# A GeGLU feed-forward kernel: the weights of contraction slice 0 in four transfers, and the opening products in another order

## The chip, the core and the metric

The kernel runs on one core of one Trainium2 chip. A core has TensorE (matrix products, PE in the profile), VectorE (DVE), ScalarE (ACT), GpSimd (POOL) and SyncE (SP), each with its own instruction stream; they meet only at semaphores. Transfers between the chip's memory (HBM) and the core's memory (SBUF) are issued by SP, ACT and POOL and run on 16 DMA engines that all queues share. Matrix products write into PSUM, which has 8 banks. The metric is the device time of one execution in microseconds; less is better.

## The reference

Input `x` is 32 x 32 x 1024, so N = 1024 tokens of D = 1024 values; `w_gate` and `w_up` are 1024 x 3584, `w_down` is 3584 x 1024, all bfloat16.

```python
def reference(x, w_gate, w_up, w_down):
    return (_gelu(x @ w_gate) * (x @ w_up)) @ w_down
```

`_gelu` is the tanh form. The first two products contract over D, the last over F = 3584.

## The kernel before

**Tiling.** D is cut into DK = 8 contraction slices of 128 (the index `dk`; "chunk" in the change's own words), F into 28 blocks of 128 (index `m`). A product instruction takes a 128 x 128 block of weights (loaded into the array by a LDWEIGHTS, PEld in the profile) and streams 128, 256 or 512 tokens of `xT`, the transposed input, through it. A *part* is one block `m` for one range of tokens; its gate product G and its up product U each sum over the 8 slices in PSUM. Parts 0 to 7 are blocks 0 to 7 for tokens 0 to 255, each with one PSUM bank of its own (G in one half, U in the other); parts 8 to 15 are the same blocks and banks for tokens 256 to 511; all parts after that are 512 tokens wide. When a part is summed, ScalarE applies the gelu to G into one of four buffers (line 443), and VectorE multiplies it with U into `hT` (line 483), which frees the bank. After the last part the down product runs (line 421).

**Opening.** The order of TensorE's instructions is a list, `steps`, written out at lines 157 to 184, and each instruction waits just for what it reads. First come ten warm-up products on constants (`WARM`, line 393: six of 512 columns, four of 128), which need no data. Then `turn_xa` (line 345) turns the first 256 tokens (two blocks `b` of 128) for slices 0 to 4: ten 128 x 128 products with an identity matrix (line 351), which go to PSUM in four pieces (`XA_PS`, line 131) and are copied to `xT` by ScalarE (line 436). VectorE turns slices 5 to 7 of the same tokens itself (line 459). Then TensorE runs slice 0 of parts 0 to 7 (line 174: G of parts 0, 1, 2, 6, 3, 7, 4, then U of 0 to 3, G of 5, U of 7, 6, 4, 5), then slices 1 to 5 of all eight parts (`together(range(0, 8), 1, 6)`), then slices 6 and 7 in two halves of four parts, slice 7 part by part so that the parts end one after another.

**Tokens 256 to 511.** Slices 0 to 3 of parts 8 to 11 are first done for tokens 256 to 383 (`XB1`), then for tokens 384 to 511 (`XB2`), because VectorE is still turning these tokens (line 474). VectorE's own order is the string `mix` at line 188: `E3` is the multiply that ends part 3, `A0` to `A3` turn slices 0 to 3 of XB1, `B` those of XB2, `D` slices 4 to 7 of both, `C` tokens 512 to 1023. VectorE, like every engine here, works strictly in that order.

**Loads.** SP issues the first 128 tokens of x, then the weights of blocks 0 to 7 as 16 transfers of 256 KB in the order gate, up for slice 0, gate, up for slice 1 and so on (`load_w0`, line 288; 128 rows of 2 KB each, one semaphore each). ACT issues the other 128 tokens. When the up weights of slice 5 have landed (line 300), SP and ACT issue the rest of x in pieces XB1, XB2 and XC2. All of SP's transfers are served by one queue in their order. The other weight blocks are loaded in groups of four blocks when the x pieces have landed or a buffer is free.

**The extra wait.** `HOLD` (line 132, used at line 379) makes U of part 6 in slice 5 wait for the gate weights of slice 7, two slices before they are read.

Of the kernel before, what the change touches and what calls it, by code (L numbers as in the profile page):

```python
# [5 lines left out]
P = 128  # L6
# [78 lines left out]
def bass_standalone__geglu_ffn__sampling_kernel(  # L85
# [13 lines left out]
    DK = D // P  # L99
# [7 lines left out]
    NBIG = 8  # L107
    GSZ = 4
# [20 lines left out]
    XB1, XB2 = (256, 384), (384, 512)  # L129
    XPIECES = [XB1, XB2, XC2]  # L130
    XA_PS = [(3, 0, 1, 0, 1), (7, 0, 1, 1, 2), (4, 1, 3, 0, 2), (5, 3, 5, 0, 2)]
    HOLD = ((6, "U", 5), ("wg", 7))
    XA_DVE = (5, 8)


# [21 lines left out]
    steps = []  # L157

    def together(ps_, k0, k1, tok=None):
        for dk in range(k0, k1):  # L160
            for key in ("G", "U"):
                for p in ps_:
                    steps.append((p, key, dk, tok))

    def one_by_one(ps_, k0):
        for p in ps_:
            for key in ("G", "U"):
                for dk in range(k0, DK):
                    steps.append((p, key, dk, None))

    for k0, k1 in ((0, 3), (3, XA_DVE[0])):
        for b in range(2):
            steps += [("X", b, dk) for dk in range(k0, k1)]
    for key, ps_ in (("G", (0, 1, 2, 6, 3, 7, 4)), ("U", (0, 1, 2, 3)), ("G", (5,)), ("U", (7, 6, 4, 5))):
        steps += [(p, key, 0, None) for p in ps_]
    together(range(0, 8), 1, 6)
    for half in (range(0, 4), range(4, 8)):
        together(half, 6, 7)
        one_by_one(half, 7)
    together(range(8, 12), 0, 4, XB1)  # L180
    together(range(8, 12), 0, 4, XB2)
    together(range(8, 12), 4, 6)
    one_by_one(range(8, 12), 6)
# [1 line left out]


    dve_order = []
    mix = ("E0 E1 E2 A0 E3 A1 A2 A3 B0 B1 B2 B3 E4 D4 D5 E5 D6 D7 E6 E7 "
           "C0 E8 C1 E9 C2 E10 E11 C3 C4 E12 C5 E13 C6 C7 E14 E15")
    for w in mix.split():  # L190
        if w[0] == "E":
# [14 lines left out]
    def evac_eng_is_act(ji):  # L206
# [9 lines left out]
    C_PE = _Clock("pe")  # L216
    C_ACT = _Clock("act")
    C_DVE = _Clock("dve")
    C_POOL = _Clock("pool")
    Q_XA = [_Clock(f"xa{b}", 16) for b in range(2)]  # L220
    Q_X = {(q, s): _Clock(f"x{i}{s}", 16) for i, q in enumerate(XPIECES) for s in range(2)}
    Q_W0 = {(w, k): _Clock(f"{w}0k{k}", 16) for k in range(DK) for w in ("wg", "wu")}
    Q_WG = [_Clock(f"wg{j}", 16) for j in range(NG)]
    Q_WU = [_Clock(f"wu{j}", 16) for j in range(NG)]
    Q_WD_SP = _Clock("wd_sp", 16)
    Q_WD_POOL = _Clock("wd_pool", 16)
    Q_OUT = _Clock("out", 16)
    all_clocks = [C_PE, C_ACT, C_DVE, C_POOL, *Q_XA, *Q_X.values(), *Q_W0.values(), *Q_WG, *Q_WU,
                  Q_WD_SP, Q_WD_POOL, Q_OUT]

    ctx = _Ctx()

    with ExitStack() as es:
        def sb(name, shape, dtype):
            return es.enter_context(nc.sbuf_tensor(name, shape, dtype))
# [9 lines left out]
        big = {w: sb(w + "big", [P, DK, NBIG * P], BF16) for w in ("wg", "wu")}  # L245
        small = {w: sb(w + "small", [P, DK, GSZ * P], BF16) for w in ("wg", "wu")}
        w_r = {"wg": wg_r, "wu": wu_r}
# [13 lines left out]
        def wbuf(w, buf):  # L261
            if buf == "s":
                return small[w]
            o = 0 if buf == "lo" else GSZ * P
            return big[w][:, :, o:o + GSZ * P]
# [15 lines left out]
        def load_x(ew, eng, q, side):  # L281
            c0, c1 = q[0] // 32, q[1] // 32
            for a in (2 * side, 2 * side + 1):
                v = ew.do(lambda: eng.dma_start(
                    xs[32 * a:32 * (a + 1), c0:c1, :], x_r[a, :, c0:c1, :]), clock=Q_X[(q, side)])
            ctx.set(("x", q, side), v)

        def load_w0(ew, eng, w, k):
            ctx.set((w + "0", k), ew.do(lambda: eng.dma_start(
                big[w][:, k, :], w_r[w][:, k, 0:NBIG * P]), clock=Q_W0[(w, k)]))  # L290

        def early_loads(ew, eng, side):
            ctx.set(("xa", side), ew.do(lambda: eng.dma_start(
                xa[:, side, :], xa_r[:, side, :]), clock=Q_XA[side]))
            yield
            if side == 0:
                for k in range(DK):
                    for w in ("wg", "wu"):
                        load_w0(ew, eng, w, k)
            ew.wait(Q_W0[("wu", 5)], ctx.get(("wu0", 5)))  # L300
            for q in XPIECES:
                load_x(ew, eng, q, side)

# [22 lines left out]
        def prog_sp(eng):  # L326
            sp = _Eng(ctx, eng, None)
            for _ in early_loads(sp, eng, 0):
                pass
            wd_mine = [k for k in range(len(wd_groups)) if k % 2 == 0]  # L330
            for j in range(NG):
                known_chunk = gate_w(sp, j)
                load_w(sp, eng, "wg", j)
                issue_wd(sp, eng, wd_mine, known_chunk, Q_WD_SP)
            issue_wd(sp, eng, wd_mine, FM, Q_WD_SP, force=True)
            ctx.set("wd_sp_total", Q_WD_SP.n)
            last = None
            for ji, (tc, col0, ncols, b) in enumerate(jobs):
                sp.wait(C_ACT if evac_eng_is_act(ji) else C_DVE, ctx.get(("E", ji)))
                last = sp.do(lambda: eng.dma_start(  # L340
                    out_r[:, tc, col0:col0 + ncols],
                    osb[:, tc, col0:col0 + ncols]), clock=Q_OUT)
            sp.wait(Q_OUT, last)
# [14 lines left out]
        def part_step(pe, eng, opened, i, key, dk, tok):  # L358
            m, t0, t1, gs, us = parts[i]
            w, (bank, f0, f1) = ("wg", gs) if key == "G" else ("wu", us)  # L360
            if tok is not None:
                f0, f1 = f0 + tok[0] - t0, f0 + tok[1] - t0
                t0, t1 = tok
            buf, slot, j = slot_of[m]
            if j is None:
                pe.wait(Q_W0[(w, dk)], ctx.get((w + "0", dk)))
            else:
                pe.wait((Q_WG if w == "wg" else Q_WU)[j], ctx.get((w, j)))
            if bank in bank_before[i]:
                pe.wait(C_DVE, ctx.get(("D", bank_before[i][bank])))  # L370
            for jx, (xbank, k0, k1, _b0, _b1) in enumerate(XA_PS):
                if t0 == XA[0] and (xbank == bank or k0 <= dk < k1):
                    pe.wait(C_ACT, ctx.get(("XA", jx)))
            if t0 == XA[0] and dk >= XA_DVE[0]:
                pe.wait(C_DVE, ctx.get("XD"))
            for q in XPIECES:
                if q[0] < t1 and t0 < q[1]:
                    pe.wait(C_DVE, ctx.get(("T", dk, q)))
            if (i, key, dk) == HOLD[0]:
                pe.wait(Q_W0[HOLD[1]], ctx.get((HOLD[1][0] + "0", HOLD[1][1])))  # L380
            first = (i, bank) not in opened
            opened.add((i, bank))
            last = (dk == DK - 1)
            v = pe.do(lambda: eng.matmul(  # L384
                ps[:, bank, f0:f1],
                wbuf(w, buf)[:, dk, slot * P:(slot + 1) * P],
                xT[:, dk, t0:t1],
                start=first, stop=last and (key == "U" or gs[0] != us[0]),
            ), mark=last)
            if last:  # L390
                ctx.set((key, i), v)

        WARM = [512] * 6 + [128] * 4

        def prog_pe(eng):
            pe = _Eng(ctx, eng, C_PE)
            for n in WARM:
                pe.do(lambda: eng.matmul(ps[:, 0, 0:n], ones_w, ones_x[:, 0:n],  # L398
# [3 lines left out]
            for step in steps:  # L402
                if step[0] == "X":
                    turn_xa(pe, eng, *step[1:])
                else:
                    part_step(pe, eng, opened, *step)
# [134 lines left out]
```

## Time and profile before

| what | value |
|---|---|
| median of 3 runs | 299.04 us (298.87 to 299.05) |
| the profiled execution | 299.08 us, of which the profile's span is 297.8 us; 1.28 us lie around it |
| TensorE products | busy 293.9 us, 99% of the span |
| LDWEIGHTS | 148.1 us, 50% (beside the products) |
| VectorE / ScalarE / GpSimd | 64.3 / 42.3 / 7.9 us |
| DMA | 26.43 MB, 89 GB/s over the span |

The profile names a group of instructions by engine, line of the code, and output and inputs. A line with "idle before" in square brackets says how long the engine was idle just ahead and what ended that. Products are pipelined: a product of 256 columns is shown for 0.27 us, but its successor starts 0.109 us later, so it is the starting times that tell the pace.

### The profile page before, as it was taken

The page shows a single profiled execution, that of the slowest core. Times are in us where ns is not written, and L with a number is a line of the kernel's source. Part 1 is how long each engine was busy: PE and PEld are TensorE (multiplying, and loading weights), DVE is VectorE, ACT ScalarE, POOL GpSimd, SP SyncE. Part 2 cuts the span into 40 slices and gives each one's busy share as a digit, 9 for nine tenths or more (in the row PEclk, how much of TensorE's full clock was granted, in tenths as well). Part 3 has the DMA queues.
Part 4 walks back from the last instruction along what each step waited for, and adds up shares of the span by engine and source line. Part 5 has one row for each costly group of instructions (what it writes and reads, how often), then busy time and mean ns, then how long its engine had stood idle before and what let it go on. Part 6 is the DMA issues. An engine that isn't in the chain of part 4 may idle for free.

```text
span 297.8 us, 3492 instructions
## 1 busy us (share of the span) xinstructions
PE 293.9 (99%) x1528; PEld 148.1 (50%) x1552; DVE 64.3 (22%) x108; ACT 42.3 (14%) x79; POOL 7.9 (3%) x14
## 2 busy tenths in 40 slices
PE   8999999999999999999999999999999999999997
PEld 5899644444444444444444444444444444444445
DVE  4669721111122111122111112110000000000000
ACT  4032211121111121111112111110000000000000
POOL 1001001020000002001000000000000000000000
PEclk9999999999999999999999999999999999999999
DMA  7997104856009301942003000000000100010001
GB/s 248 392 207 233 52 2 139 284 199 227 0 0 298 127 0 34 371 161 110 33 0 141 0 2 0 0 0 20 18 18 20 35 18 18 20 35 18 18 20 35
DMA packets 17806, 26.43 MB, mean 89 GB/s; under 512 B 1152, under 2 KB 11392, under 8 KB 17792
## 3 DMA queue, kind: packets, MB, share of 16 engines
q1 hardware_dynamic: 13840, 16.78, 17.0%
q0 software_dynamic: 2176, 8.39, 7.8%
q10 hardware_dynamic: 1776, 1.05, 1.5%
q8 instruction: 12, 0.20, 0.3%
q14 instruction: 2, 0.02, 0.0%
HBM read 24.12 MB, written 2.10 MB: 88 GB/s over the span
## 4 chain that ended last, share of the span: by engine, by line
PE 99%; issue 0%; ACT 0%
PE ps L384 65%; PE ps L421 32%; PE ps L398 1%; PE ps L351 0%; ACT xT L449 0%
## 5 line engine op out<-in xcount | busy, mean ns | idle before, releaser
L421 PE MATMUL ps<-wd,hT 128*128 128x512 bf16 (+2 forms) x468 | 96.5, 366 | 0.4
L384 PE MATMUL ps<-xT,wubig 128*128 128x512 bf16 (+2 forms) x395 | 79.5, 336 | 0.3
L384 PE MATMUL ps<-xT,wgbig 128*128 128x512 bf16 (+2 forms) x394 | 79.1, 336 | 0.3
L421 PEld LDWEIGHTS ps<-wd,hT 128*128 128x128 bf16 x476 | 45.5, 98 | 51.6
L483 DVE TENSOR_TENSOR hT<-tb,ps 128x512 bf16<-128x512 f32 (+1 forms) x64 | 38.8, 613 | 136.3 <-PE ps L384 131.7
L443 ACT ACTIVATE tb<-ps 128x512 f32<-128x512 f32 (+1 forms) x64 | 34.2, 544 | 158.1 <-PE ps L384 157.9
L384 PEld LDWEIGHTS ps<-xT,wubig 128*128 128x128 bf16 x400 | 38.1, 98 | 31.6 <-DMA wubig<-in_w_up_dram 0.3
L384 PEld LDWEIGHTS ps<-xT,wgbig 128*128 128x128 bf16 x400 | 38.0, 98 | 31.5 <-DVE xT L474 0.2
L384 PE MATMUL ps<-xT,wgsmall 128*128 128x512 bf16 x126 | 30.1, 379 | 0.1
L384 PE MATMUL ps<-xT,wusmall 128*128 128x512 bf16 x125 | 29.8, 379 | 0.2
L489 DVE CAST xT<-ps 128x512 bf16<-128x512 f32 (+1 forms) x8 | 5.4, 675 | 89.6 <-PE ps L421 89.6
L384 PEld LDWEIGHTS ps<-xT,wusmall 128*128 128x128 bf16 x128 | 12.5, 98 | 15.1
L384 PEld LDWEIGHTS ps<-xT,wgsmall 128*128 128x128 bf16 x128 | 12.5, 98 | 15.1
L449 ACT ACTIVATE xT<-ps 128x512 bf16<-128x512 f32 (+1 forms) x9 | 5.1, 562 | 93.1 <-PE ps L421 93.1
L474 DVE STREAM_TRANSPOSE xT<-hT 128x128 bf16<-128x128 bf16 (+2 forms) x20 | 13.3, 701 | 0.0
L459 DVE STREAM_TRANSPOSE xT<-hT 32x192 bf16<-32x192 bf16 x16 | 8.2, 515 | 4.7 <-DMA hT<-in_x_dram 4.3
L278 POOL DMA_DIRECT2D wubig<-in_w_up_dram x3 | 2.7, 886 | 62.6 <-PE ps L384 62.6
L398 PE MATMUL ps<-const-bfloat16-1.0 128*128 128x512 bf16 (+1 forms) x10 | 3.1, 498 | 0.8 <-PEq L526 0.8
L278 POOL DMA_DIRECT2D wusmall<-in_w_up_dram x2 | 2.0, 992 | 47.8 <-PE ps L384 26.0
L272 POOL DMA_DIRECT2D wd<-in_w_down_dram x3 | 2.3, 764 | 19.1 <-PE ps L384 19.1
L398 PEld LDWEIGHTS ps<-const-bfloat16-1.0 128*128 128x128 bf16 x10 | 1.2, 139 | 2.4 <-issue 2.4
L436 ACT ACTIVATE xT<-ps 128x128 bf16<-128x128 f32 (+1 forms) x4 | 1.6, 436 | 2.1 <-PE ps L351 2.0
(10 smaller groups left out, 4.8 us busy)
## 6 DMA issues: line engine op xcount, KB each, us to landing
wd<-in_w_down_dram SPq DMA_DIRECT2D x4, 1024.0 KB, 11.4
wgbig<-in_w_gate_dram SPq DMA_DIRECT2D x3, 1024.0 KB, 5.8
wubig<-in_w_up_dram POOLq DMA_DIRECT2D x3, 1024.0 KB, 9.7
wd<-in_w_down_dram POOLq DMA_DIRECT2D x3, 1024.0 KB, 11.4
wgbig<-in_w_gate_dram SPq DMA_DIRECT2D x8, 256.0 KB, 5.7
wubig<-in_w_up_dram SPq DMA_DIRECT2D x8, 256.0 KB, 5.9
wgsmall<-in_w_gate_dram SPq DMA_DIRECT2D x2, 1024.0 KB, 6.1
wusmall<-in_w_up_dram POOLq DMA_DIRECT2D x2, 1024.0 KB, 9.9
```

The lines of the kernel that those rows point to most:

```text
L272: ew.do(lambda: eng.dma_start(wd[:, a:b, :], wd_r[:, a:b, :]), clock=clock)
L278: ctx.set((w, j), ew.do(lambda: eng.dma_start(wbuf(w, buf)[:, :, 0:gsz * P], w_r[w][:, :, c0 * P:(c0 + gsz) * P]), clock=q))
L384: v = pe.do(lambda: eng.matmul(ps[:, bank, f0:f1], wbuf(w, buf)[:, dk, slot * P:(slot + 1) * P], xT[:, dk, t0:t1], start=first, stop=last ...
L398: pe.do(lambda: eng.matmul(ps[:, 0, 0:n], ones_w, ones_x[:, 0:n], start=True, stop=True), mark=False)
L421: v = pe.do(lambda: eng.matmul(ps[:, b, 0:ncols], hT[:, m, tc * P:(tc + 1) * P], wd[:, m, col0:col0 + ncols], start=(m == 0), stop=(m == F ...
L436: ctx.set(("XA", j), act.do(lambda: eng.activation(xT[:, k0:k1, P * b0:P * b1], ps[:, bank, 0:nt * (k1 - k0)].rearrange("p (k t) -> p k t" ...
L443: ctx.set(("A", i), act.do(lambda: eng.activation(t_bufs[i % NTB][:, 0:t1 - t0], ps[:, gb, g0:g1], ACTF.Gelu_apprx_tanh)))
L449: ctx.set(("E", ji), act.do(lambda: eng.activation(osb[:, tc, col0:col0 + ncols], ps[:, b, 0:ncols], ACTF.Copy)))
L459: v = dve.do(lambda: eng.transpose(xT[32 * a:32 * (a + 1), XA_DVE[0]:XA_DVE[1], XA[0]:XA[1]].rearrange("p k (b t) -> p k b t", t=P)[:, :, ...
L474: v = dve.do(lambda: eng.transpose(xT[:, dk, q[0]:q[1]].rearrange("p (c i) -> p c i", i=32), src))
L483: ctx.set(("D", i), dve.do(lambda: eng.tensor_tensor(hT[:, m, t0:t1], t_bufs[i % NTB][:, 0:t1 - t0], ps[:, ub, u0:u1], ALU.mult)))
L489: ctx.set(("E", ji), dve.do(lambda: eng.tensor_copy(osb[:, tc, col0:col0 + ncols], ps[:, b, 0:ncols])))
```

## The change

1. **Four transfers for slice 0.** The gate and up weights of slice 0 are loaded as two halves each: gate of blocks 0 to 3, gate of 4 to 7, up of 0 to 3, up of 4 to 7, 128 KB each with rows of 1 KB. Slices 1 to 7 stay as they were. SP issues 18 transfers in place of 16, and each slice-0 product waits for its half. The order of slice-0 gate products becomes 0, 1, 2, 3, 6, 7, 4.
2. **Turning order.** The ten turning products go block 0 slices 0 and 1, block 1 slices 0 and 1, then slices 2 to 4 of each (before: slices 0 to 2 of each, then 3 and 4).
3. **Slices 6 and 7.** The order becomes: slice 6 of parts 0 to 3; G of slice 6 of parts 4 to 7; slice 7 of parts 0 to 3; U of slice 6 of parts 4 to 7; slice 7 of parts 4 to 7. `HOLD` is gone.
4. **Tokens 256 to 383.** Slices 0 and 1 are done for parts 8 to 10, then for part 11, then slices 2 and 3 for all four.
5. **VectorE's order.** `A0` stands ahead of `E0`, and `A1` ahead of `E3`.
6. **Warm-up.** One more product of 128 columns.

No product of the computation is added or left out.

```diff
-    HOLD = ((6, "U", 5), ("wg", 7))
+    W0 = [(w, 0, m, m + GSZ) for w in ("wg", "wu") for m in (0, GSZ)]
+    W0 += [(w, k, 0, NBIG) for k in range(1, DK) for w in ("wg", "wu")]
+    w0_of = {(w, k, m): i for i, (w, k, m0, m1) in enumerate(W0) for m in range(m0, m1)}
+    W0_GATE = w0_of[("wu", 5, 0)]
...
-    for k0, k1 in ((0, 3), (3, XA_DVE[0])):
+    for k0, k1 in ((0, 2), (2, XA_DVE[0])):
         for b in range(2):
             steps += [("X", b, dk) for dk in range(k0, k1)]
-    for key, ps_ in (("G", (0, 1, 2, 6, 3, 7, 4)), ("U", (0, 1, 2, 3)), ("G", (5,)), ("U", (7, 6, 4, 5))):
+    for key, ps_ in (("G", (0, 1, 2, 3, 6, 7, 4)), ("U", (0, 1, 2, 3)), ("G", (5,)), ("U", (7, 6, 4, 5))):
         steps += [(p, key, 0, None) for p in ps_]
     together(range(0, 8), 1, 6)
-    for half in (range(0, 4), range(4, 8)):
-        together(half, 6, 7)
-        one_by_one(half, 7)
-    together(range(8, 12), 0, 4, XB1)
+    together(range(0, 4), 6, 7)
+    steps += [(p, "G", 6, None) for p in range(4, 8)]
+    one_by_one(range(0, 4), 7)
+    steps += [(p, "U", 6, None) for p in range(4, 8)]
+    one_by_one(range(4, 8), 7)
+    together(range(8, 11), 0, 2, XB1)
+    together(range(11, 12), 0, 2, XB1)
+    together(range(8, 12), 2, 4, XB1)
     together(range(8, 12), 0, 4, XB2)
...
-    mix = ("E0 E1 E2 A0 E3 A1 A2 A3 B0 B1 B2 B3 E4 D4 D5 E5 D6 D7 E6 E7 "
+    mix = ("A0 E0 E1 E2 A1 E3 A2 A3 B0 B1 B2 B3 E4 D4 D5 E5 D6 D7 E6 E7 "
...
-        def load_w0(ew, eng, w, k):
-            ctx.set((w + "0", k), ew.do(lambda: eng.dma_start(
-                big[w][:, k, :], w_r[w][:, k, 0:NBIG * P]), clock=Q_W0[(w, k)]))
+        def load_w0(ew, eng, i):
+            w, k, m0, m1 = W0[i]
+            ctx.set(("w0", i), ew.do(lambda: eng.dma_start(
+                big[w][:, k, m0 * P:m1 * P], w_r[w][:, k, m0 * P:m1 * P]), clock=Q_W0[i]))
...
-            ew.wait(Q_W0[("wu", 5)], ctx.get(("wu0", 5)))
+            ew.wait(Q_W0[W0_GATE], ctx.get(("w0", W0_GATE)))
...
-            if (i, key, dk) == HOLD[0]:
-                pe.wait(Q_W0[HOLD[1]], ctx.get((HOLD[1][0] + "0", HOLD[1][1])))
...
-        WARM = [512] * 6 + [128] * 4
+        WARM = [512] * 6 + [128] * 5
```

More of the change, by code (lines that the diff above doesn't have):

```diff
@@ L221, in bass_standalone__geglu_ffn__sampling_kernel @@
     Q_X = {(q, s): _Clock(f"x{i}{s}", 16) for i, q in enumerate(XPIECES) for s in range(2)}
-    Q_W0 = {(w, k): _Clock(f"{w}0k{k}", 16) for k in range(DK) for w in ("wg", "wu")}
+    Q_W0 = [_Clock(f"w0n{i}", 16) for i in range(len(W0))]
     Q_WG = [_Clock(f"wg{j}", 16) for j in range(NG)]
@@ L227, in bass_standalone__geglu_ffn__sampling_kernel @@
     Q_OUT = _Clock("out", 16)
-    all_clocks = [C_PE, C_ACT, C_DVE, C_POOL, *Q_XA, *Q_X.values(), *Q_W0.values(), *Q_WG, *Q_WU,
+    all_clocks = [C_PE, C_ACT, C_DVE, C_POOL, *Q_XA, *Q_X.values(), *Q_W0, *Q_WG, *Q_WU,
                   Q_WD_SP, Q_WD_POOL, Q_OUT]
@@ L296, in early_loads @@
             if side == 0:
-                for k in range(DK):
-                    for w in ("wg", "wu"):
-                        load_w0(ew, eng, w, k)
-            ew.wait(Q_W0[("wu", 5)], ctx.get(("wu0", 5)))
+                for i in range(len(W0)):
+                    load_w0(ew, eng, i)
+            ew.wait(Q_W0[W0_GATE], ctx.get(("w0", W0_GATE)))
             for q in XPIECES:
@@ L365, in part_step @@
             if j is None:
-                pe.wait(Q_W0[(w, dk)], ctx.get((w + "0", dk)))
+                pe.wait(Q_W0[w0_of[(w, dk, m)]], ctx.get(("w0", w0_of[(w, dk, m)])))
             else:
```

## The prediction

> **What bounds the kernel now.** I read the busy times first, then the chain of work that ended last, then the waits of TensorE's weight loads, and last the loads' issue and landing times. The busy row of the page and the beginning of the chain (start, length, what):
>
> ```profile
> PE 293.9 (99%) x1528; PEld 148.1 (50%) x1552; DVE 64.3 (22%) x108; ACT 42.3 (14%) x79; POOL 7.9 (3%) x14
> ...
> 0.76 3.15 PE ps L398 x10
> 3.91 1.13 PE ps L351 x10
> 5.03 0.92 PE ps L384 x7
> ...
> 5.97 27.45 PE ps L384 x281
> ```
>
> TensorE sets the time from end to end: warm-up, turning, then products without a hole to the end (the rest of the chain is PE too). So only idle or slow time of TensorE can be won, and there is little. The two waits of its product weight loads, and the weight loads of the opening:
>
> ```profile
> PEld ps L384 <- DMA wubig<-in_w_up_dram: 0.3, 1, 0.3
> PEld ps L384 <- DVE xT L474: 0.2, 1, 0.2
> ...
> 3.86 1.04 PEld L351 LDWEIGHTS ps<-ident,hT 128*128 128x128 bf16 x10 [0.22 <-issue]
> 5.01 0.66 PEld L384 LDWEIGHTS ps<-xT,wgbig 128*128 128x128 bf16 x7
> 5.97 0.33 PEld L384 LDWEIGHTS ps<-xT,wubig 128*128 128x128 bf16 x4 [0.30 <-DMA wubig<-in_w_up_dram]
> ...
> 6.42 0.42 PEld L384 LDWEIGHTS ps<-xT,wubig 128*128 128x128 bf16 x4
> 6.89 0.82 PEld L384 LDWEIGHTS ps<-xT,wgbig 128*128 128x128 bf16 x8
> ```
>
> The reader is to see one stall that counts: the up weights of slice 0, 0.30 us. (The wait for L474 does not count: the product rows around it start at 19.19, 19.41, 19.64, with four products of 0.056 us each time, so the products did not pause.) Now the loads: SP's queue, then the landing of the first three transfers after their issue at 1.17, 1.63 and 2.10 us (last number, in us):
>
> ```profile
> 1.17 0.42 SPq L289 DMA_DIRECT2D wgbig<-in_w_gate_dram  x1
> 1.63 0.42 SPq L289 DMA_DIRECT2D wubig<-in_w_up_dram  x1
> 2.10 0.43 SPq L289 DMA_DIRECT2D wgbig<-in_w_gate_dram  x1
> ...
> wgbig<-in_w_gate_dram SPq DMA_DIRECT2D x1, 256.0 KB, 3.8
> ...
> wubig<-in_w_up_dram SPq DMA_DIRECT2D x1, 256.0 KB, 4.3
> ...
> wgbig<-in_w_gate_dram SPq DMA_DIRECT2D x1, 256.0 KB, 4.8
> ```
>
> They land at 4.97, 5.93 and about 6.9. All three are just in time: the first gate product starts at 5.01, the first up product at 5.97, and slice 1's gate weights are taken at 6.89, where the previous weight load had ended at 6.84. After that the loads run ahead (the up weights of slice 1, issued at 2.58, land at 7.6 and are needed at 7.73; from there one lands each 0.7 us, and TensorE takes 8 products of 0.109, 0.87 us, for each). So slice 1's gate weights are a second limit, 0.07 us behind the first: the products of slice 0 end at 6.96.
>
> **The change, part by part.**
>
> *Four transfers for slice 0.* The first up product can start on half the bytes, so the 0.30 us stall ahead of it goes, and the first gate product (now at 5.01, held by its weights at 4.97) could start when the turned tokens are there, about 4.9. Without that stall, slice 0 (16 products at 0.109 = 1.75 us) would end at 4.93 + 1.75 = 6.68 to 5.01 + 1.75 = 6.76. What is late next is slice 1's gate weights, whose landing depends on all bytes ahead of them, and those are the same. So TensorE waits there, until 6.89 at best.
>
> What the two more transfers cost SP: 0.47 us of issue each, so slice 1 is issued at 3.04 in place of 2.10. That is covered by the queue: its data came after 4.8 us of which most was waiting for earlier bytes. At 0.47 us for 128 KB the issue feeds 279 GB/s, and the engines drew 351 GB/s between 2.50 and 6.80, but half a megabyte of x stands ahead of it. Slice 0's last half is issued at 2.58; slice 1 would be late only if the bytes ahead of it were gone by about 4.1 (its issue and the 1.04 us that the first x transfer took from issue to the first data, an estimate from the window in which data starts), and they are gone at about 5.9.
>
> Rows of 1 KB in place of 2 KB: the nearest rows are stretches in which the engines were full with the one and the other.
>
> ```profile
> 9.00:10.50 1.50, 1.50 (x16) 1.34 (x15) 1.41 (x4) 0.00 (x0) 0.00 (x0) 1.00 1.06 407
> 26.00:27.50 1.50, 1.50 (x16) 1.34 (x15) 1.50 (x4) 0.77 (x2) 0.00 (x0) 1.00 1.09 380
> 2.50:6.80 4.30, 4.28 (x32) 2.93 (x31) 2.42 (x5) 1.58 (x4) 0.00 (x0) 1.00 1.01 351
> ```
>
> The last number is GB/s. The first stretch carries rows of 2 KB, the second only rows of 1 KB. Slice 0 is 0.524 MB: 1.380 us at 380, 1.288 at 407, so +0.09 us. I take that: slice 1's gate weights are usable at 6.98. Its first product starts there in place of 6.96: **+0.02 us**. Bounds: if halving the rows costs nothing, 6.89, so -0.07. Below that, if smaller pieces use the engines better in the opening (351 GB/s against 407 later: 4.30 x (1 - 351/407) = 0.59 us at most), slice 1 is there before TensorE, and slice 0's own end decides, 6.68: -0.28. Above, by the x pieces of 512 B (205 GB/s between 16 and 22 us, in part idle, so too high a price): 1 KB at the middle of 407 and 205, 306 GB/s, gives 1.713 - 1.288 = +0.43, so usable at 7.32 and +0.36.
>
> The Trainium skill, page "DMA: Bandwidth & Descriptors", section "Why small descriptors are slow (HBM only)", speaks against this part: a fixed cost of about 3 cycles for each packet beside one cycle for each 32 bytes. For 1 KB that is 35 cycles for 32, for 2 KB 67 for 64, so by the page alone an estimate of 4.5% or 0.06 us, and the sum would be -0.01 in place of +0.02. The two stretches agree in sign, with 6.6%.
>
> *Gate order 0, 1, 2, 3, 6, 7, 4; turning order.* The same instructions. Block 1's first turning product, the fourth before, becomes the third, due at about 4.09, but block 1's tokens (issued by ACT at 0.78, 3.4 us to landing) come at 4.15 to 4.2: up to 0.11 us of waiting, and the third and fourth copy of ScalarE start up to 0.27 later because two more turning products stand ahead of each. Part 4's gate product needs the third copy and may wait 0.1 us. The whole is covered by the wait for slice 1 (6.76 + 0.1 is still below 6.98); were that cover gone, it would cost up to 0.2. **0.**
>
> *Warm-up.* One more of 128 columns, 0.107 us (the 512 ones start 0.427 apart). It fills the idle 0.22 us of the weight loads at 3.86, where TensorE waits for x (issued at 0.72, 3.0 us to landing). **0**; up to +0.1 if x came earlier, and then covered by slice 1.
>
> *HOLD and the order of slices 6 and 7.* The held product ran at about 15.4; the weights it waits for were issued at 8.48 and landed 6.5 later, 14.98. It did not wait, so taking it out gives **0**; if the loads came 0.4 later it would have. Four gate products more stand between slices 6 and 7, so slice 7's up weights (15.85) are needed at 17.0 in place of 16.57. Parts 0 to 3 end 0.44 us later, parts 4 to 7 as before.
>
> *VectorE's order.* Its rows now:
>
> ```profile
> 17.56 1.08 DVE L483 TENSOR_TENSOR hT<-tb,ps 128x256 bf16<-128x256 f32 x3 [4.60 <-ACT tb L443]
> 18.56 0.40 DVE L474 STREAM_TRANSPOSE xT<-hT 128x128 bf16<-128x128 bf16 x1
> 18.88 0.38 DVE L483 TENSOR_TENSOR hT<-tb,ps 128x256 bf16<-128x256 f32 x1
> 19.18 2.14 DVE L474 STREAM_TRANSPOSE xT<-hT 128x128 bf16<-128x128 bf16 x7
> ```
>
> Part 0 ends 0.44 later, its gelu at about 17.8, so VectorE would idle; `A0` fills that. Its tokens were issued at 13.36 and 13.39 and landed at 17.3 and 17.5; with +0.09 `A0` starts at 17.6. With the rows' spacing (0.32, then 0.33 each) `E0` to `E2` start at 17.9, 18.25, 18.6, `A1` at 18.9, `E3` 19.25, `A2` 19.55, `A3` 19.85. TensorE needs `E2` at 19.3 (ends 19.0), `A1` at 19.53 (19.3), `E3` at 19.86 (19.65), `A2` at 20.09 (19.95). Each holds; the tightest by 0.1. **0.** If x came 0.25 later, each 0.1 more would cost 0.1.
>
> **Sum:** +0.02 us on the profiled execution's 299.08 (0.04 above the median, within the runs' spread): 299.1 us.
>
> **The rivals.**
> *Slice 1 lands earlier* (faster): slice 0 in smaller pieces lifts the opening's 351 GB/s. For it: the rate is below 407. Against: the engines were busy all along (share 1.01), so there is no idle to fill. 298.8.
> *The halves cost more than the late rows say*, by the upper bound: 299.45.
> *The clock steps up late* (slower): the warm-up and turning products run at half pace (512 columns in 0.427 us, against twice 0.109 later), the first gate products at full pace, so the step came between 4.2 and 5.0, some 4 us after the first product. If the new pause in the turning makes that count begin anew at 3.86, it comes at about 7.9; from 5.0 products take 0.213, 13.6 are done by then, the other 2.4 end at 8.16 in place of 6.96: +1.2, 300.3 us. It decides from the pause that is too long; 0.2 us was not, and the longer warm-up shortens that one. Against it too: three runs within 0.18 us. The page "TensorE: Matmul & The Clock Gate" of the Trainium skill, Part 1 on the HAM clock gate, has the window run free, 3.4 us long, so that the step would move from run to run; the spread of the runs speaks against much of that.
> *VectorE behind late x* (slower): x lands later than 17.8 and `A0` holds up `E0` to `E2`, and so the banks of parts 8 to 10. For a loss of 0.6 us x must come 0.85 later than now, ten times the delay worked out: 299.7.
>
> **How the numbers follow.** Forecast (stall moves to slice 1; -0.1 to +0.2) 0.64; slice 1 earlier 0.14; costlier halves 0.11; clock 0.07; VectorE 0.04. A measurement of this kernel can tell about 0.2%, 0.6 us, from no change. Slower by more: clock, VectorE, and 0.03 of the costlier halves, 0.14. Faster by more: nothing visible is that large; 0.05, out of the second case, for what these rows do not show. Same: 0.81. The range leaves these two ends out: 298.7 to 299.8.
>
> **What would show it.** No wait before the first up product, and a wait of 0.1 to 0.3 us of slice 1's first weight load for its gate weights, at about 6.95; full pace from then on with no hole around 19 to 21 us. The forecast is wrong if that wait is missing, if the first products start more than 0.109 us apart, or if a weight load waits for VectorE for over 0.2 us.

## The result and the profile after

The changed kernel takes 300.39 us (median of 8 runs, 299.81 to 301.02) against 299.15 us (298.87 to 299.51) for the kernel before in runs on the same chip. The ratio is 1.0042, 95% interval 1.0029 to 1.0056: 1.2 us slower, outside the range given. In a second comparison of the same two kernels, among the experiments below, it was 1.0036 [1.0024, 1.0048].

The profiled execution of after took 300.96 us with a span of 299.6 us, 1.88 us more than the 299.08 us of the one before; it is one of the longer ones of its kernel (0.57 us over the median), so the account that follows is of a larger loss than the usual one. The page's busy row, and the chain of work that ended last (start, length, what), of the kernel after:

```profile
PE 296.1 (99%) x1553; PEld 148.3 (50%) x1553; DVE 64.2 (21%) x108; ACT 42.5 (14%) x79; POOL 7.9 (3%) x14
```

```profile
3.05 4.65 DMA wgbig<-in_w_gate_dram
7.70 0.05 issue
7.74 12.43 PE ps L389 x112
20.17 0.05 issue
20.22 0.20 DVE hT L488
20.42 0.13 issue
20.55 0.42 DVE hT L488
20.97 0.05 issue
21.02 180.03 PE ps L389 x926
201.05 96.78 PE ps L426 x476
```

Before, the chain was TensorE alone from 0.76 us on. Now it runs through a DMA and through VectorE, and both places lie in the first 21 us. What follows is as long as before: the down product starts at 201.05 in place of 199.18, which is 1.87 of the 1.88 us. (PE's busy time rose by 2.2 us, but with 25 more products on record where the change adds one: some records were missing before, so this row doesn't measure the loss.)

TensorE's waits in the kernel after (us in total, times, longest):

```profile
PEld ps L389 <- DVE hT L488: 0.9, 3, 0.5
PEld ps L389 <- DMA wgbig<-in_w_gate_dram: 0.8, 1, 0.8
...
PEld ps L389 <- DVE xT L479: 0.3, 1, 0.3
```

The wait for the up weights of slice 0 is gone, as forecast. Three others stand in its place. The weight loads around them, in the same kernel:

```profile
4.89 1.07 PEld L389 LDWEIGHTS ps<-xT,wgbig 128*128 128x128 bf16 x7
5.98 0.43 PEld L389 LDWEIGHTS ps<-xT,wubig 128*128 128x128 bf16 x4
...
6.52 0.42 PEld L389 LDWEIGHTS ps<-xT,wubig 128*128 128x128 bf16 x4
7.74 0.77 PEld L389 LDWEIGHTS ps<-xT,wgbig 128*128 128x128 bf16 x8 [0.79 <-DMA wgbig<-in_w_gate_dram]
```

```profile
20.35 0.10 PEld L389 LDWEIGHTS ps<-xT,wgbig 128*128 128x128 bf16 x1 [0.48 <-DVE hT L488]
20.68 0.10 PEld L389 LDWEIGHTS ps<-xT,wgbig 128*128 128x128 bf16 x1 [0.24 <-DVE hT L488]
21.01 0.10 PEld L389 LDWEIGHTS ps<-xT,wgbig 128*128 128x128 bf16 x1 [0.23 <-DVE hT L488]
```

The account of the 1.87 us by the starting times of TensorE's weight loads: slice 1 starts at 7.74 in place of 6.89, **+0.85**. (This compares one execution with one; in later profiles of kernels that lose nothing slice 1 starts at up to 7.54, so most of this step need not be the change's own. The table at the end of the experiments shows which part is.) The first products of parts 8, 9 and 10 wait for their banks, which VectorE frees at L488: **+0.92** more. The rest, about 0.1, is the wait for L479. VectorE's own rows say why it was late (kernel after, 19 to 22 us):

```profile
19.59 0.41 DVE L479 STREAM_TRANSPOSE xT<-hT 128x128 bf16<-128x128 bf16 x1 [6.70 <-DMA hT<-in_x_dram]
19.92 1.04 DVE L488 TENSOR_TENSOR hT<-tb,ps 128x256 bf16<-128x256 f32 x3
20.88 0.40 DVE L479 STREAM_TRANSPOSE xT<-hT 128x128 bf16<-128x128 bf16 x1
```

`A0`, which the change put first, waited 6.70 us for tokens of XB1 that came at 19.5, and `E0` to `E2` stood behind it although their inputs were there. Those tokens are issued when slice 5's up weights have landed. SP's queue, first before, then after:

```profile
1.17 0.42 SPq L289 DMA_DIRECT2D wgbig<-in_w_gate_dram  x1
1.63 0.42 SPq L289 DMA_DIRECT2D wubig<-in_w_up_dram  x1
2.10 0.43 SPq L289 DMA_DIRECT2D wgbig<-in_w_gate_dram  x1
...
12.98 3.50 SPq L284 DMA_DIRECT2D hT<-in_x_dram  x6
```

```profile
1.17 0.89 SPq L297 DMA_DIRECT2D wgbig<-in_w_gate_dram  x2
2.10 0.91 SPq L297 DMA_DIRECT2D wubig<-in_w_up_dram  x2
3.05 0.43 SPq L297 DMA_DIRECT2D wgbig<-in_w_gate_dram  x1
...
14.12 3.94 SPq L291 DMA_DIRECT2D hT<-in_x_dram  x6
```

The third row of each is slice 1's gate weights, issued at 2.10 and at 3.05. The last row is the first x piece: it shows slice 5 landing 1.14 us later, though the same bytes were to be moved and slice 0's last half was there at 5.7 us, sooner than before (5.93). The engines had work all the time and moved less. Two stretches of before, then three of after (the last columns are the granted clock, the share of DMA engines busy, and GB/s):

```profile
5.00:8.00 3.00, 2.98 (x27) 2.40 (x27) 2.85 (x6) 0.86 (x2) 0.00 (x0) 1.00 0.98 341
8.00:11.00 3.00, 3.00 (x30) 2.69 (x28) 2.81 (x7) 0.00 (x0) 0.00 (x0) 1.00 1.05 404
```

```profile
5.00:8.00 3.00, 2.49 (x21) 1.86 (x20) 2.83 (x6) 1.08 (x2) 0.00 (x0) 1.00 0.95 288
8.00:11.00 3.00, 3.00 (x30) 2.60 (x28) 2.82 (x6) 0.00 (x0) 0.00 (x0) 1.00 0.95 324
11.00:14.00 3.00, 3.00 (x30) 2.69 (x29) 1.80 (x4) 0.00 (x0) 0.00 (x0) 1.00 1.05 396
```

From 8 to 11 us both kernels move the same kind of transfer, 256 KB with rows of 2 KB, and after moves a fifth less of it. From 11 to 14 us the rate is 396 GB/s again.

So three questions were left: whether the four transfers alone do this, by which of their properties (the rows of 1 KB, or the two more issues), and whether the new orders of TensorE and VectorE add a part of their own.

### The profile page after: what moved, and what is told of

It is laid out like the page before. It is cut to its first block, busy times and chain, and to the rows that moved or that the text cites. A ratio compares the mean times of both kernels' runs of the same rounds, so it can differ in the third digit from the quotient of the medians.

```text
span 299.6 us, 3519 instructions
## 1 busy us (share of the span) xinstructions
PE 296.1 (99%) x1553; PEld 148.3 (50%) x1553; DVE 64.2 (21%) x108; ACT 42.5 (14%) x79; POOL 7.9 (3%) x14
## 4 chain that ended last, share of the span: by engine, by line
PE 97%; DMA 2%; SPq 1%; DVE 0%; issue 0%; ACT 0%
PE ps L389 64%; PE ps L426 32%; DMA wgbig<-in_w_gate_dram 2%; SPq L297 1%; DVE hT L488 0%; SPq L301 0%; ACT xT L454 0%
## 5 line engine op out<-in xcount | busy, mean ns | idle before, releaser
L389 PE MATMUL ps<-xT,wgbig 128*128 128x512 bf16 (+2 forms) x400 | 80.6, 338 | 0.9 <-DMA wgbig<-in_w_gate_dram 0.5
L488 DVE TENSOR_TENSOR hT<-tb,ps 128x512 bf16<-128x512 f32 (+1 forms) x64 | 38.8, 612 | 131.7 <-PE ps L389 131.7
L479 DVE STREAM_TRANSPOSE xT<-hT 128x128 bf16<-128x128 bf16 (+2 forms) x20 | 13.4, 702 | 6.7 <-DMA hT<-in_x_dram 6.7
```

What stands on the lines that cost most here:

```text
L389: v = pe.do(lambda: eng.matmul(ps[:, bank, f0:f1], wbuf(w, buf)[:, dk, slot * P:(slot + 1) * P], xT[:, dk, t0:t1], start=first, stop=last ...
L479: v = dve.do(lambda: eng.transpose(xT[:, dk, q[0]:q[1]].rearrange("p (c i) -> p c i", i=32), src))
L488: ctx.set(("D", i), dve.do(lambda: eng.tensor_tensor(hT[:, m, t0:t1], t_bufs[i % NTB][:, 0:t1 - t0], ps[:, ub, u0:u1], ALU.mult)))
```

## The experiments

Each is compared with the kernel before. "x issued" is the time of SP's first x issue in the profile, that is, when slice 5's up weights had landed: 12.98 us before, 14.12 after.

**The changed kernel with slice 0 in two transfers.**

```diff
-    W0 = [(w, 0, m, m + GSZ) for w in ("wg", "wu") for m in (0, GSZ)]
+    W0 = [(w, 0, 0, NBIG) for w in ("wg", "wu")]
```

> The changed kernel with slice 0 in two transfers of 256 KB again, all else as changed. Theory T (the four transfers make the loads of slice 1 and after late, and the late x is then made dear by VectorE's new order): slice 1's gate weights usable at about 6.9, XB1 landed by 17.6, no wait of a weight load for VectorE over 0.2 us; 299.2 us, ratio to before 0.999 to 1.001. Rival V (VectorE's order and the order of the slice 6 and 7 products lose the time by themselves): 300.2 us, ratio 1.003 to 1.005. Rival C (the longer warm-up and the new turning order move the step of the clock): still a late step, 299.6 to 300.4.

Ratio 0.9997 [0.9988, 1.0006]. x issued at 12.73; no weight load waits for a DMA. All of the loss hangs on the split.

**The kernel before with the four transfers alone** (and the order 0, 1, 2, 3, 6, 7, 4 of the gate products, without which the split is of little use).

```diff
+    W0 = [(w, 0, m, m + GSZ) for w in ("wg", "wu") for m in (0, GSZ)]
...
-    for key, ps_ in (("G", (0, 1, 2, 6, 3, 7, 4)), ("U", (0, 1, 2, 3)), ("G", (5,)), ("U", (7, 6, 4, 5))):
+    for key, ps_ in (("G", (0, 1, 2, 3, 6, 7, 4)), ("U", (0, 1, 2, 3)), ("G", (5,)), ("U", (7, 6, 4, 5))):
```

> The kernel before with slice 0 in four transfers (and the gate order 0, 1, 2, 3, 6, 7, 4 that goes with them) and nothing else. T: slice 1's gate weights usable at about 7.7 in place of 6.9, so 0.8 us lost there, of which nothing comes back, and x 1 to 2 us late, of which VectorE's old order lets less through: 299.8 to 300.3 us, ratio 1.0025 to 1.004. V and C: as before, 299.15 us, ratio 0.999 to 1.001.

Ratio 1.0021 [1.0009, 1.0033]; x issued at 13.71. The split alone makes the kernel slower, and by another stall than after's. In this kernel's weight loads slice 1 came in time, and slice 7's up weights did not:

```profile
17.18 0.10 PEld L388 LDWEIGHTS ps<-xT,wgbig 128*128 128x128 bf16 x1
18.18 0.10 PEld L388 LDWEIGHTS ps<-xT,wubig 128*128 128x128 bf16 x1 [0.90 <-DMA wubig<-in_w_up_dram]
```

Its stretch from 8 to 11 us is as slow as after's:

```profile
8.00:11.00 3.00, 3.00 (x30) 2.67 (x29) 2.81 (x7) 0.00 (x0) 0.00 (x0) 1.00 0.99 317
```

What is common to the two is the low rate; where TensorE meets it differs. The low rate is not all of this stall, though: slice 7's up weights landed 2.4 us behind its gate weights (0.9 us in before), and they did so by 2.2 to 2.4 us in three kernels with slice 1 issued at 2.10, too (TensorE's order alone, turning and warm-up alone, and the changed kernel with the up halves from ACT). What makes that last gap long is open.

**VectorE's order: the old one in the changed kernel, and the new one in the kernel before.** The first:

```diff
-    mix = ("A0 E0 E1 E2 A1 E3 A2 A3 B0 B1 B2 B3 E4 D4 D5 E5 D6 D7 E6 E7 "
+    mix = ("E0 E1 E2 A0 E3 A1 A2 A3 B0 B1 B2 B3 E4 D4 D5 E5 D6 D7 E6 E7 "
```

> The changed kernel with VectorE's order as before (E0 E1 E2 A0 E3 A1). T: slice 1 still late by 0.8 us, but parts 8 to 10 wait only for A0 and not for E0 to E2 behind it: 0.3 to 0.9 us less than the changed kernel, 299.6 to 300.0 us, ratio 1.0015 to 1.003. V: all comes back, 299.2 us. If VectorE's order does not matter at all: 300.4 us.

Ratio 1.0031 [1.0019, 1.0042], against 1.0042 and 1.0036 with the new order: not to be told apart. In its profile the waits for L488 are gone, but TensorE waits 0.9 us for slice 7's up weights and 0.7 us for VectorE's turning in their place. The 0.7 us need not come of late x: the same 0.7 us in three waits stands in the profile of TensorE's new order alone, below, where x was issued at 13.04, and 0.2 to 0.4 us where both new orders are in place. Whether the order adds a part within the changed kernel stays open. The second is the same edit the other way round, in the kernel before:

> The kernel before with VectorE's new order and nothing else. T: x lands at 17.45 as before, so A0 ends at about 17.9 and E2 at about 19.0, and parts 8 to 10 lose 0 to 0.2 us: 299.2 us, ratio 0.999 to 1.001. V: 299.9 to 300.3 us, ratio 1.003 to 1.004.

Ratio 1.0002 [0.9993, 1.0011]: with x in time (XB1 landed at 17.66) no cost shows. One wait in this profile matters for reading the others. The opening and the loads are those of before, slice 1 is issued at 2.11, and yet its gate weights came late:

```profile
7.50 0.77 PEld L384 LDWEIGHTS ps<-xT,wgbig 128*128 128x128 bf16 x8 [0.50 <-DMA wgbig<-in_w_gate_dram]
```

So a wait at slice 1 in a single execution does not need the split.

**The new order of TensorE's products alone** (slices 6 and 7, parts 8 to 11, no `HOLD`) in the kernel before.

```diff
-    HOLD = ((6, "U", 5), ("wg", 7))
...
-    for half in (range(0, 4), range(4, 8)):
-        together(half, 6, 7)
-        one_by_one(half, 7)
-    together(range(8, 12), 0, 4, XB1)
+    together(range(0, 4), 6, 7)
+    steps += [(p, "G", 6, None) for p in range(4, 8)]
+    one_by_one(range(0, 4), 7)
+    steps += [(p, "U", 6, None) for p in range(4, 8)]
+    one_by_one(range(4, 8), 7)
+    together(range(8, 11), 0, 2, XB1)
+    together(range(11, 12), 0, 2, XB1)
+    together(range(8, 12), 2, 4, XB1)
```

> The kernel before with the new order of slices 6 and 7, of tokens 256 to 383, and without HOLD; nothing else. Theory T (only the four transfers cost, directly and by the late x): ratio to before 0.999 to 1.001. Rival: these orders hold the remaining 0.3 us by which the changed kernel with VectorE's old order (ratio 1.0031) is above the four transfers alone (1.0021): ratio 1.001.

Ratio 1.0006 [0.9997, 1.0015]: no difference that the interval shows. The profile has 0.7 us of waits for VectorE's turning (0.2 in before), so with VectorE's old order a small cost is possible.

**The turning order and the warm-up alone** in the kernel before.

```diff
-    for k0, k1 in ((0, 3), (3, XA_DVE[0])):
+    for k0, k1 in ((0, 2), (2, XA_DVE[0])):
...
-        WARM = [512] * 6 + [128] * 4
+        WARM = [512] * 6 + [128] * 5
```

> The kernel before with the new turning order and the longer warm-up, nothing else. T: block 1's first turning product waits 0.1 us for x, covered by the wait for slice 0's up weights; ratio 0.999 to 1.001. Rival C: the pause moves the step of the clock, ratio 1.001 to 1.004.

Ratio 0.9999 [0.9990, 1.0008]. TensorE's weight loads paused 0.22 us for block 1's tokens, where up to 0.11 was worked out, and no cost shows. (In this profile slice 7's up weights made TensorE wait 0.32 us, with x issued at 12.63: that wait does not need late loads either.)

**Four transfers with rows of 2 KB.** Slice 0 is halved by partitions, 64 rows of 2 KB each, in the kernel with the four transfers alone. A product then waits for both halves, so nothing can start early; what it tests is whether the rows of 1 KB are to blame.

```diff
-    W0 = [(w, 0, m, m + GSZ) for w in ("wg", "wu") for m in (0, GSZ)]
+    W0 = [(w, 0, q, q + P // 2) for w in ("wg", "wu") for q in (0, P // 2)]
...
-                big[w][:, k, m0 * P:m1 * P], w_r[w][:, k, m0 * P:m1 * P]), clock=Q_W0[i]))
+                big[w][q0:q1, k, :], w_r[w][q0:q1, k, 0:NBIG * P]), clock=Q_W0[i]))
```

> The kernel before with slice 0 in four transfers that are halves by partitions (64 rows of 2 KB each) in place of halves by blocks (128 rows of 1 KB); each slice-0 product waits for both halves. Theory N (the two more issues on SP put slice 1 and all after it 0.94 us later into the queue, and the engines, with less queued ahead, run slower than 400 GB/s until about 11 us): the up weights of slice 5 land at 13.4 to 13.8 as with the four transfers by blocks, ratio 1.0015 to 1.003. Rival R (the rows of 1 KB disturb what follows, the issue does not matter): they land at 12.7 to 13.0 as in the kernel before, ratio 0.999 to 1.0007.

Ratio 1.0044 [1.0030, 1.0058]; x issued at 14.89. No row is shorter than before, and the stretch is the slowest of all:

```profile
8.00:11.00 3.00, 3.00 (x21) 2.35 (x20) 2.84 (x6) 0.00 (x0) 0.00 (x0) 1.00 0.97 289
```

SP's issues took longer in this form (slice 1's gate weights issued at 3.66), so it isn't a clean repeat of the four transfers. Its products also wait for both halves, so the time lost is not that of the rate alone. But the low rate does not need rows of 1 KB.

**The two halves of the up weights issued by ACT.** The four transfers of 128 KB stay, and SP issues 16 transfers as before; slice 1 is issued at 2.10 again, and the two halves go out on ACT from 1.2 us on. Once in the kernel with the four transfers alone, once in the changed kernel in full.

```diff
+            if side == 1:
+                for i in (2, 3):
+                    load_w0(ew, eng, i)
             yield
             if side == 0:
                 for i in range(len(W0)):
-                    load_w0(ew, eng, i)
+                    if i not in (2, 3):
+                        load_w0(ew, eng, i)
```

> The kernel before with slice 0 in four transfers by blocks (rows of 1 KB), of which ACT issues the two up halves behind its x transfer, so that SP issues slice 1 at 2.1 us as in the kernel before. N: no long slow stretch, slice 1's gate weights usable by 6.7, the up weights of slice 5 by 12.9, ratio 0.998 to 1.000, the fastest so far. R: as with the four transfers on SP, 13.4 to 13.8 and ratio 1.0015 to 1.003.

> The changed kernel in full, but ACT issues the two up halves of slice 0 behind its x transfer, so that SP issues slice 1 at 2.1 us. N: all of the loss goes, VectorE's and TensorE's new orders cost nothing once x lands by 17.8: ratio 0.998 to 1.0005. Rival (the orders keep a part): 1.001 to 1.002.

Ratios 0.9998 [0.9990, 1.0007] and 0.9998 [0.9989, 1.0006]; x issued at 12.61 and 12.99. The whole loss is gone in both, with rows of 1 KB and with all the new orders in place. SP's queue in the changed kernel with this edit, and the same two stretches (the group of three is slice 0's two gate halves and slice 1's gate weights):

```profile
1.17 1.37 SPq L297 DMA_DIRECT2D wgbig<-in_w_gate_dram  x3
2.58 0.43 SPq L297 DMA_DIRECT2D wubig<-in_w_up_dram  x1
```

```profile
5.00:8.00 3.00, 3.00 (x24) 2.39 (x22) 2.84 (x6) 1.08 (x2) 0.00 (x0) 1.00 0.97 344
8.00:11.00 3.00, 3.00 (x30) 2.69 (x28) 2.81 (x7) 0.00 (x0) 0.00 (x0) 1.00 1.06 409
```

The engines move 344 and 409 GB/s again. This edit does two things at once, though: slice 1 and the up halves are issued sooner, and the early bytes stand in two queues. The next run takes the time of the issue by itself.

**The kernel before, with slice 1 issued late.** The same 16 transfers; SP waits ahead of slice 1 for two spare operations of GpSimd.

```diff
                 for k in range(DK):
+                    if k == 1:
+                        ew.wait(C_POOL, ctx.get("late"))
...
+            for n in range(2):
+                v = pool.do(lambda: eng.tensor_scalar(
+                    spare[n][:, :], diff[:, :], 0.0, None, ALU.is_equal))
+            ctx.set("late", v)
```

> The kernel before with the same 16 transfers of 256 KB, but SP waits before the first transfer of slice 1 for two small extra operations of GpSimd on spare memory, which end at about 2.8 us; so slice 1 is issued at about 2.9 in place of 2.10 us and nothing else differs. Theory N (what is queued ahead decides; the late issue alone makes the engines slow): rate under 370 GB/s until about 11 us, up weights of slice 5 landed at 13.3 to 13.8, ratio to before 1.0015 to 1.003. Rival M (more transfers, not later ones, are the cost): landed at 12.7 to 13.0, ratio 0.9995 to 1.0005.

Slice 1 was issued at 2.70, 0.60 us late, and x at 13.49. The stretches of this kernel:

```profile
5.00:8.00 3.00, 3.00 (x25) 2.45 (x24) 2.84 (x6) 0.99 (x2) 0.00 (x0) 1.00 0.99 358
8.00:11.00 3.00, 3.00 (x30) 2.69 (x29) 2.81 (x7) 0.00 (x0) 0.00 (x0) 1.00 1.02 333
```

333 GB/s from 8 to 11 us, with no transfer added or cut, against 399 to 409 in all eight profiles with slice 1 issued at 2.10: a late issue by itself lowers the rate of transfers that start long after it. The time hardly followed: 1.0010 [0.9998, 1.0021], with one wait of 0.27 us for slice 7's up weights in the profile, and 3 of 11 runs at 300.3 to 300.6 us. This is less than was expected. The delay is 0.60 where the change makes 0.95, and loads that need about 0.7 us each against 0.87 us of products have some slack to eat up first; that this explains the difference is argued, not shown. So this run shows the low rate to come from the late issue, and leaves open how much of the change's time does.

**The kernel before, slices 2 to 7 loaded in pairs** of 512 KB, 10 issues in place of 16, to see whether more bytes queued early make the engines faster.

```diff
+    K0 = (0, 1, 2, 2, 4, 4, 6, 6)
...
+            k1 = k + K0.count(k)
             ctx.set((w + "0", k), ew.do(lambda: eng.dma_start(
-                big[w][:, k, :], w_r[w][:, k, 0:NBIG * P]), clock=Q_W0[(w, k)]))
+                big[w][:, k:k1, :], w_r[w][:, k:k1, 0:NBIG * P]), clock=Q_W0[(w, k)]))
```

> The kernel before with slices 2 to 7 loaded in pairs, two slices of one matrix in a transfer of 512 KB: 10 issues in place of 16, slices 0 and 1 as before. N: more is queued from 3.05 us on, so the slow stretch (under 390 GB/s until about 8 us) ends by about 7, the weights of slice 5 land at 12.3 to 12.6 in place of 12.97; TensorE waits for nothing there, so the time stays, ratio 0.999 to 1.0005. If the queue's depth does not matter: slow until 8, slice 5 at 12.9 or later.

A miss: 1.0014 [1.0004, 1.0023]. Its rates are those of the kernel before (346 and 406 GB/s), so more queued bytes did not lift them, and a pair is ready only when all of it has landed, so slice 2 waits:

```profile
10.10 0.77 PEld L386 LDWEIGHTS ps<-xT,wubig 128*128 128x128 bf16 x8 [0.59 <-DMA wubig<-in_w_up_dram]
```

**The changed kernel once more**, unaltered, beside the others.

> The changed kernel once more. N: again a slow stretch until about 11 us, up weights of slice 5 at 13.4 to 14.2, waits of TensorE's weight loads of 0.5 us or more in sum, for weights of slice 1 or 7 or for VectorE behind late x; ratio 1.003 to 1.0055, about 300.5 us.

Ratio 1.0036 [1.0024, 1.0048]; x issued at 14.29, 335 GB/s from 8 to 11 us. In this execution slice 1's gate weights caused no wait. Slice 2's did:

```profile
8.32 0.86 PEld L389 LDWEIGHTS ps<-xT,wubig 128*128 128x128 bf16 x8
9.66 0.77 PEld L389 LDWEIGHTS ps<-xT,wgbig 128*128 128x128 bf16 x8 [0.48 <-DMA wgbig<-in_w_gate_dram]
```

Put side by side, the rate falls into two groups without overlap. "Slice 1 landed" is its gate weights; the next to last column is the first weight load of TensorE for tokens 384 to 511, which comes behind every wait named so far:

| kernel | slice 1 issued by SP (us) | slice 1 landed (us) | GB/s, 8 to 11 us | x issued (us) | tokens 384 to 511 begin (us) | ratio to before |
|---|---|---|---|---|---|---|
| before | 2.10 | 6.85 | 404 | 12.98 | 20.93 | 1 |
| after, slice 0 in two | 2.10 | 6.68 | 404 | 12.73 | 21.43 | 0.9997 |
| four transfers, up halves from ACT | 2.10 | 6.51 | 399 | 12.61 | 21.29 | 0.9998 |
| after, up halves from ACT | 2.11 | 6.98 | 409 | 12.99 | 21.61 | 0.9998 |
| VectorE's order alone | 2.11 | 7.45 | 404 | 13.54 | 21.47 | 1.0002 |
| TensorE's order alone | 2.10 | 6.98 | 401 | 13.04 | 21.77 | 1.0006 |
| turning and warm-up alone | 2.10 | 6.51 | 406 | 12.63 | 21.13 | 0.9999 |
| slices 2 to 7 in pairs | 2.11 | 6.45 | 406 | 12.79 | 21.45 | 1.0014 |
| before, slice 1 late | 2.70 | 6.44 | 333 | 13.49 | 21.51 | 1.0010 |
| four transfers alone | 3.05 | 6.47 | 317 | 13.71 | 22.44 | 1.0021 |
| after, VectorE's old order | 3.06 | 6.89 | 321 | 13.69 | 22.78 | 1.0031 |
| after | 3.05 | 7.70 | 324 | 14.12 | 22.80 | 1.0042 |
| after, again | 3.05 | 7.31 | 335 | 14.29 | 22.37 | 1.0036 |
| four transfers by partitions | 3.66 | 7.52 | 289 | 14.89 | 23.33 | 1.0044 |

Slice 1's landing hardly sorts by its issue; the rate behind it does. By the time TensorE takes tokens 384 to 511, the four kernels with the 128 KB transfers all on SP stand at 22.4 to 22.8 us and those with slice 1 issued at 2.10 at 20.9 to 21.8.

## Why the prediction was wrong

**The step that failed is "What the two more transfers cost SP", priced at nothing with the words "That is covered by the queue".** That step asked only whether slice 1's gate weights would still stand in line in time, and let the loads behind them run ahead whatever the issue did. For slice 1 the answer can't be called wrong: its weights landed at 6.47 to 7.70 us in the four kernels with the 128 KB transfers all on SP and at 6.45 to 7.45 where SP issued them on time, so the 7.70 of after is no measure of the late issue. What the step left out is everything behind slice 1: from 8 to 11 us the loads ran at 317 to 335 GB/s in place of 399 to 409, and slice 5 landed, and x was issued, at 13.7 to 14.3 in place of 12.6 to 13.5. Whether the queue runs empty before the next issue was the wrong test: the run with one late issue and unchanged transfers shows the rate falling with the engines busy (shares 0.99 and 1.02). Moving the two issues to ACT takes the whole loss away, which makes this term the one that was mis-sized: **0 forecast, 1.1 to 1.3 us measured** (1.0036 to 1.0042 with it, 0.9998 without, so 0.0038 to 0.0044 of 299.5; the intervals allow about 0.4 us either way). Shown is that the two more issues on SP's queue cost this; that it is their delay alone, and not that the pieces share one queue, is not, since the delay alone gave 1.0010 [0.9998, 1.0021].

The Trainium skill, page "DMA: Bandwidth & Descriptors", section "Issuing engines are not separate DMA queues", holds that issuing from several engines saves no more than the sequencer's time, usually small beside the transfer. The sequencer's time saved here is 0.95 us, and the time of the kernel moved by about as much, within the intervals. "Small" does not fit transfers of this size: 0.47 us of issue for each, where in before one of 256 KB landed each 0.7 us.

**Where the stall goes.** "TensorE waits there", at slice 1's gate weights, held for the profiled execution: the wait for slice 0's up weights is gone, the wait for slice 1 is there. Its size was forecast at 0.1 to 0.3 us and was 0.79. It isn't bound to that place: in the repeat it was slice 2, in three other kernels with a late issue slice 7's up weights. These are the places where the loads, which I had as running ahead, have the least margin in before: 0.04 and 0.2 us at slice 1, 0.4 and 0.6 at slice 2, 0.7 at slice 7's up weights, and 0.8 to 1.9 in between (`HOLD` aside). Which one a single execution meets is in part chance: kernels with slice 1 issued on time had waits of 0.50 us at slice 1 and of 0.32 at slice 7 as well.

**Rows of 1 KB, +0.09 us.** Not seen: with them, and with SP's issues restored, the ratio is 0.9998. The rival of costlier halves is refuted by the same run. A small cost, such as the 0.09 us of the two stretches or the 0.06 us weighed beside it, is below what these runs can tell.

**Gate order, turning order, warm-up, `HOLD`, slices 6 and 7: 0.** Right as far as the intervals tell, each about 0.1% wide to either side: 0.9999 for the turning and warm-up alone, 1.0006 for the steps alone, and all of them together at 0.9998.

**VectorE's order, 0, and the rival "VectorE behind late x".** The price of 0 is right where x comes in time (1.0002 alone; 0.9998 in the changed kernel with the up halves on ACT, where XB1 landed at 18.02, past the 17.8 set as the limit, and no weight load waited for a multiply). In the profiled execution of after the rival came true by its own mechanism: it was to decide from x later than 17.8 us, x came at 19.5, and TensorE lost 0.92 us at parts 8 to 10. I gave it 0.04 since the delay had to be ten times what I had worked out. Both delays were taken as independent small sums; in fact both hang on the same two issues: these make slices 2 to 5 late, and x is issued only after slice 5. The case was a consequence of the failed step and should not have had a chance of its own. How much the order adds in a typical execution is open, as said above.

**Slice 1 earlier, as a faster rival.** Not borne out: with SP's issues restored the two kernels with four transfers have 384 and 344 GB/s from 5 to 8 us, and slice 1 landed at 6.51 and 6.98. Kernels with slice 0 in two transfers show 341 to 373 GB/s and 6.45 to 7.45, so what the pieces win, if anything, is within the scatter, and both ratios are 0.9998.

**The clock.** The step from half to full pace does move from one execution to the next. The first seven gate products took 0.92 us in before's chain, 1.70 in two other profiles, and in that of the four transfers alone 1.68:

```profile
5.19 1.68 PE L388 MATMUL ps<-xT,wgbig 128*128 128x256 bf16 x7
```

That agrees with the Trainium skill, page "TensorE: Matmul & The Clock Gate", Part 1, on a window that runs free. A late step costs single executions about as much as the stall at slice 1: in the changed kernel with the up halves on ACT the seven products took 1.70 us, and slice 1 started at 7.54 with no wait for its weights. It is no cause of the loss, since that kernel's ratio is 0.9998, and with the longer warm-up and the changed turning alone the time stayed at 0.9999. My mechanism (a pause beginning the count anew) was not seen: in that last run the turning paused 0.22 us, and the seven products took 0.96. But the three runs within 0.18 us, which I held against a moving step, were too few: 28 runs of before range from 298.87 to 300.53 us. How much of that the step makes was not separated.

**What stays open** is why the engines move less when slice 1 comes 0.6 to 0.95 us later. The rows' length is excluded, and the depth of the queue in bytes found no support in the run with pairs. The packets in the traces narrow it down: of the 2 KB packets that start between 8 and 11 us the median took 84 ns in before, in after and in the run with slice 1 late alike, but the longest took 156, 569 and 480 ns. In all eight kernels with slice 1 issued on time the longest was at most 258 ns, in all six with a later issue at least 480. So the rate falls mostly by a few long packets, and not by all of them taking longer; what holds those few is not known. None of the versions tried is faster than the kernel before: with the up halves on ACT the 0.30 us stall at slice 0 is gone too, and the time is the same, 0.9998.

## What to carry to other kernels

Splitting a transfer is not free for the queue that issues it: each of these pieces took 0.47 us of SP, and everything behind was issued later. Don't take "there are still bytes ahead of it" as proof that a later issue is covered; look at the rate by stretch and at the landing of the last transfer that something else waits for, and if a split is wanted, issue the extra pieces from a queue that is idle (here that lost nothing, and gained nothing either). Don't take the place of a stall in one profile for its cause: kernels that ran equally fast started slice 1 at 6.85 to 7.54 us here. Where an engine works strictly in order, putting work that depends on a load at the front ties everything behind it to that load, and two small risks that hang on one queue are one risk.

## What the runs showed of the hardware that was not expected

- One issue 0.60 us late lowered the rate between 8 and 11 us to 333 GB/s (399 to 409 in eight kernels with the issue on time), although all of these transfers were issued by SP well ahead of their landing; from 11 to 14 us it was 391 again. The median 2 KB packet took 84 ns all the same; a few took up to 480.
- Slice 0 in four transfers with rows of 1 KB, issued in time, showed no cost beyond the scatter: 345 and 371 GB/s from 2.50 to 6.80 us, against 351 to 367 in six kernels with two transfers and rows of 2 KB.
- The pace of TensorE's products steps up at a time that differs between executions: the first seven gate products took between 0.92 and 1.70 us.
